# Windowed attention and a softplus FFN on one core: three score passes per head pair and query tile instead of four, and two buffers moved

## The chip, the cores and the metric

The kernel runs on one core of a Trainium2 chip. The metric is the device time of one execution in microseconds (us); lower is better. The engines are TensorE (PE in the profile; PEld are its weight loads), VectorE (DVE), ScalarE (ACT), GpSimd (POOL) and SyncE (SP), whose queue issues the DMAs. A pass is one matmul instruction: a weight load of up to 128 columns and a stream of moving columns over it.

## The reference

Attention over a causal window of 64 positions, followed by two matrix products with a softplus between them. Inputs are float32: q, k and v are (8, 8, 576, 64), that is 8 sequences, 8 heads, 576 positions, 64 per head; w_in is (512, 2048) and w_out (2048, 512).

```python
scores = scale * np.matmul(q, k.transpose(0, 1, 3, 2))
mask = (rel >= 0) & (rel < window)            # rel = query position - key position, window = 64
scores = np.where(mask, scores, -1000000000.0)
scores = scores - np.max(scores, axis=-1, keepdims=True)
attn = np.exp(scores)
attn = attn / (np.sum(attn, axis=-1, keepdims=True) + 1e-09)
attn_out = np.matmul(attn, v)
...
x = np.ascontiguousarray(attn_out.transpose(0, 2, 1, 3)).reshape(B * S, H * D)   # 4608 x 512
h = x @ w_in
g = np.maximum(h, 0.0) + np.log1p(np.exp(-np.abs(h)))
return (g @ w_out).astype(np.float32)
```

## The kernel before, in words

**Tiles.** The 4608 rows are cut into 12 blocks of 384 (TB), a block into 3 query tiles of 128 rows (NJ), the 8 heads into 4 head pairs of 2 x 64 = 128 rows of the transposed q and k. For a query tile only 192 keys can matter (W): 64 before it and its own 128.

**Two parts for one float32.** Most passes run on a type of 4 bytes that TensorE reads at less than float32's precision (fp32r). The kernel therefore writes a float32 value as an upper part (the value converted) and a lower part (the difference), and adds up the products of the parts that matter: upper x upper, upper x lower, lower x upper. The feed-forward passes (`ffn_up`, L401, and `ffn_down`, L422) do so with three passes for each product.

**Scores (L258).** In the first two blocks (`by_pe`) one float32 pass over a block diagonal of k (kbd, L113) gives the scores of both heads. In the ten later blocks q_hl holds, for each head of the pair, q's upper part in partitions 0 to 63 and q's lower part in 64 to 127 (L236, L237; q_in is loaded so that both halves hold the head). k_hi and k_lo (L242, L243) hold the head's k in both halves. One pass with q_hl of a head as weights and k_hi of the head as moving columns gives upper x upper + lower x upper; one with k_lo gives the terms with k's lower part. That is two passes of 192 columns for a head, four for a tile, 12 for a head pair of a block.

**After the scores.** VectorE adds the mask and takes the minimum (L265), folds the columns (L271), ScalarE takes the exponentials (L275), VectorE normalizes (L280 to L283). The weights are cut into bf16 parts (L303 to L311) and transposed by two DMAs (L307, L312) into tr. v is loaded into v_in (L318) and cut into three bf16 parts, v12 and v13 (L324, L325, L327, L328, L329). Then attention times v runs in short bf16 passes (L376), once for each head; the first half of a head's passes reads v12, the second v13. ScalarE and VectorE add the two halves of the result into xf (L381, L382), and xf is cut into x's two parts (L384, L385), which the feed-forward network of that block reads.

**Feed-forward.** For each of 16 slices of 128 hidden columns, `ffn_up` makes 12 passes of 384 columns into one of two PSUM tiles (ps_h), ScalarE and VectorE compute the softplus (L405, L406, L407, L409) and its two parts g (L411, L412); `ffn_down` makes 9 passes of 512 columns into the three output tiles.

**Order of the work.** `attention` is a generator that yields between its stages. Each stage of each head pair, each `ffn_up` and each `ffn_down` gets a due time, and all are emitted in the order of the due times (L448 to L478). Step n of the feed-forward network has 2n + 0.5 for its up part and 2n + 5.5 for its down part; 16 steps make a block, so a block has 32 units. A head pair of a late block starts 8 units after the one before it (SHP), and STG (L30) gives the times of its stages from there: -13 loads of q and k, -5.9 q_hl, -5 k_hi and k_lo, 0, 1, 2 the scores of the three tiles, 3 to 7 the softmax and the transposes, 7.1 the load of v_in, 12 and 14 its conversion, 16 and 17 attention times v for the two heads, xf and x. So the stages 16 and 17 of one head pair are due at 8 and 9 of the next. From due time 100 on TensorE runs in the order of emission; the order on the other engines and on SP's queue is made by the framework's scheduler, which need not keep it. The head pairs of block 2 (the third) start 7 units apart.

**Buffers.** Tiles with the same tag share a buffer, and the next tile of a tag waits until the last reader of the one before it is done. Here k_hi and k_lo take the tags k0 and k1 (shared with kbd), v_in the tag v_in (shared with the weights converted last, L160), xf the tag xf (shared with the identity matrix ident of the transposes, L140), q_hl the tag q_hl (shared with pt). Each has one buffer.

Of the kernel before, what the change touches and what calls it, by code (L numbers as in the profile page):

```python
# [8 lines left out]
F32 = mybir.dt.float32  # L9
BF16 = mybir.dt.bfloat16  # L10
F32R = mybir.dt.float32r
U32 = mybir.dt.uint32
AF = mybir.ActivationFunctionType
ALU = mybir.AluOpType

P = 128
TB = 384
NJ = TB // P
# [8 lines left out]
BASE = (-100, -10, 24)  # L27
PACE = (5, 4, 7)
STG0 = (-4.5, 0.5, 1, 2, 3, 4, 7, 8)
STG = (-13, -5.9, -5, 0, 1, 2, 3, 4, 5, 6, 7, 7.1, 12, 14, 16, 17)  # L30
SH, SHP = -12, 8
PE_ORDERED_FROM = 100
MANUAL = {mybir.EngineType.PE}
# [6 lines left out]
def window_attention_softplus_ffn(  # L40
# [7 lines left out]
    S: int,  # L48
    D: int,
):  # L50

# [13 lines left out]
    nc = tc.nc  # L65
# [13 lines left out]
    att = ctx.enter_context(tc.tile_pool(name="att", bufs=1))  # L79
# [29 lines left out]
    W = CH + P  # L109

    kbd_s = [att.tile([P, 2, CH + TB], F32, name="kbd", tag=f"k{i}") for i in range(2)]  # L113
    for t in kbd_s:
        nc.gpsimd.memset(t[D:P, 0, :], 0.0)
        nc.gpsimd.memset(t[0:D, 1, :], 0.0)
        nc.gpsimd.memset(t[0:D, 0, 0:CH], 0.0)
        nc.gpsimd.memset(t[D:P, 1, 0:CH], 0.0)

    v13 = cpool.tile([P, NCH, 2, 2, D], BF16, name="v13")  # L120
    v_ts = [att.tile([P, 2, NJ, P], F32, name="v_t", tag=n) for n in ("nat", "tr")]
    for t in v_ts:
        nc.gpsimd.memset(t[0:CH, 0, 0, :], 0.0)

# [12 lines left out]
    mask_c = cpool.tile([P, W], BF16, name="mask_c")  # L137
    nc.gpsimd.tensor_copy(mask_c, mask)
    nc.gpsimd.memset(mask_c[:, 0:CH], FAR)
    ident = att.tile([P, P], F32, name="ident", tag="xf")  # L140
    make_identity(nc, ident)

    mask_b = cpool.tile([P, W], BF16, name="mask_b")
# [4 lines left out]
    mm, tp = nc.tensor.matmul, nc.tensor.transpose  # L148
# [34 lines left out]
    def attention(g, hp):  # L183
# [36 lines left out]
        if by_pe:  # L220
            v_t = v_ts[hp % 2]

            def load_v(rows, lay, j0, j1, start):
                n = rows.stop - rows.start
                src = v[start + j0 * P : start + j1 * P, c0 : c0 + P].rearrange("(j p) n -> p j n", p=P)
                nc.sync.dma_start(v_t[rows, lay, j0:j1, :], src[:n, :, :])

            if t0 == 0:
                nc.sync.dma_start(v_t[CH:P, 0, 0, :], v[0:CH, c0 : c0 + P])
            load_v(slice(0, P), 0, 1 if t0 == 0 else 0, NJ, t0 - CH)  # L230
            load_v(slice(0, CH), 1, 0, NJ, t0 + CH)
            load_v(slice(CH, P), 1, 0, NJ, t0)
        else:
            q_hl = att.tile([P, 2, TB], F32R, name="q_hl")
            low = heads[1]
            nc.scalar.copy(q_hl, q_in)  # L236
            nc.vector.tensor_tensor(  # L237
                q_hl[low, :, :], q_in[low, :, :], q_hl[low, :, :].bitcast(F32), ALU.subtract
            )
            yield  # L240
            k_hi, k_lo = [att.tile([P, 2, W - P + TB], F32R, name=f"k{i}") for i in range(2)]
            nc.scalar.copy(k_hi, k_in)  # L242
            nc.vector.tensor_tensor(k_lo, k_in, k_hi.bitcast(F32), ALU.subtract)  # L243
        yield

        st = att.tile([P, 2, NJ, W], F32, name="st", bufs=2)
# [2 lines left out]
        for j in range(NJ):  # L249
            sp = bank()  # L250
            spv = sp[:, : 2 * W].rearrange("p (h c) -> p h c", h=2)
            js, kc = slice(j * P, (j + 1) * P), slice(j * P, j * P + W)
            if by_pe:
                mm(spv, qf[:, js], kf[:, :, kc], start=True, stop=True)  # L254
            else:
                for hh in range(2):
                    for i, part in enumerate((k_hi, k_lo)):
                        mm(  # L258
                            spv[:, hh, :], q_hl[:, hh, js], part[:, hh, kc],
                            start=(hh == 0 and i == 0), stop=(hh == 1 and i == 1), skip_group_check=True,  # L260
                        )
            t = ORDER[g] * NJ + j
            m = mask_c if (t * P) % S == 0 else mask_b if (t * P) % S + P > S else mask
            for hh in range(2):
                nc.vector.tensor_tensor_reduce(  # L265
                    st[:, hh, j, :], spv[:, hh, :], m, QSCALE, 3.0e38, ALU.add, ALU.min, mn[:, hh, j : j + 1]
                )
            yield
# [3 lines left out]
        for hh in range(2):  # L272
            for j in range(NJ):
                i = hh * NJ + j
# [8 lines left out]
        nc.vector.tensor_tensor(pn, pn, sm.unsqueeze(2).to_broadcast([P, 2 * NJ, P]), ALU.mult)  # L283
        if by_pe:

            pt = att.tile([P, 2, TB], F32, name="pt", tag="q_hl")
            for hh in range(2):
                pp = bank()
                for j in range(NJ):
                    tp(pp[:, j * P : (j + 1) * P], sv[:, hh * NJ + j, 0:P], ident)  # L290
                (nc.vector.tensor_copy if hh else nc.scalar.copy)(pt[:, hh, :], pp[:, :TB])
        else:

            nat = att.tile([P, 2, 4 * NJ, 2, CH], BF16, name="nat")
            tr = att.tile([P, 8 * NJ, P], BF16, name="tr")
# [14 lines left out]
            nc.vector.tensor_tensor(part(1, 0), pv[0], part(0, 1), ALU.subtract)  # L310
            nc.vector.tensor_copy(nat[:, 1, :, 1, :], nat[:, 0, :, 0, :])  # L311
            nc.sync.dma_start(  # L312
                tr[:, n:, :], nat[:, 1, :, :, :].rearrange("p n b c -> p (n b c)"), transpose=True
            )
            yield
            v_in = att.tile([P, NCH, P], F32, name="v_in")
            for half in heads:
                nc.sync.dma_start(v_in[half, :, :], v[ks, c0 : c0 + P].rearrange("(c p) n -> p c n", p=CH))  # L318
            yield

            v12 = att.tile([P, NCH, 2, 2, D], BF16, name="v12")
            vv = v_in.rearrange("p c (h d) -> p c h d", h=2)
            up, low = heads
            nc.scalar.copy(v12[:, :, :, 0, :], vv)  # L324
            nc.vector.tensor_tensor(vv, vv, v12[:, :, :, 0, :], ALU.subtract)  # L325
            yield
            nc.scalar.copy(v12[:, :, :, 1, :], vv)  # L327
            nc.vector.tensor_tensor(v13[low, :, :, 0, :], vv[low, :, :, :], v12[low, :, :, 1, :], ALU.subtract)  # L328
            nc.vector.tensor_copy(v13[up, :, :, 0, :], v12[up, :, :, 0, :])  # L329
# [8 lines left out]
        if by_pe:  # L338
            av = bank()
        else:  # L340
            xf = att.tile([P, TB], F32, name="xf")
            trf = tr.rearrange("p n t -> p (n t)")
        for hh in range(2):
            if by_pe:
                for a in range(2 * NJ):
# [3 lines left out]
                        start=(a == 0), stop=(a == 2 * NJ - 1), skip_group_check=True,  # L349
# [8 lines left out]
            for s in range(2):  # L358
                for c in range(0 if prev else 1, NCH):


                    j = (c - 1) // 2
                    n = s * 4 * NJ + (hh * NJ + j) * 2
# [11 lines left out]
            for i, (s, c, src, osl) in enumerate(passes):  # L375
                mm(  # L376
                    av[:, osl], (v13 if s else v12)[:, c, hh, :, :], src,
                    start=(i == 0), stop=(i == len(passes) - 1), skip_group_check=True,
# [12 lines left out]
    part = {}  # L391
# [131 lines left out]
```

## Time and profile before

| | |
|---|---|
| median of 3 runs | 1031.11 us (1030.70 to 1031.97) |
| the profiled execution, its own time | 1030.02 us |
| its span | 1028.2 us |
| mean granted TensorE clock | 0.976 |
| busy share of the span: PE, PEld, DVE, ACT, POOL | 95%, 84%, 78%, 72%, 6% |
| score passes L258 | 480 of 128x192, 76.5 us busy |
| feed-forward passes L401, L422 | 2304 and 1728, 445.3 and 435.5 us busy |
| attention times v, L376 | 1088 |

A row of instructions reads: line, engine, operation, written tile <- read tiles, shape and type, count, then busy time in us and the mean of one in ns, then the idle time of the engine just before them and what ended most of it. Matmuls overlap in time, so the mean of one pass is longer than the distance between the starts of two. A timeline row reads: start in us from the start of the span, duration in us, engine, line, operation, tiles, shape, and how many instructions the row merges. SPq is SP's queue, on which DMAs are issued. A row of waits reads: who waited for whom, us in total, times, the longest.

### The profile page before, as it was taken

Reading aid. Unit: us, or ns where it says so; the run is one execution under the profiler, and the core shown is the slowest. Engines: PE = TensorE matmul, PEld = TensorE weight load, DVE = VectorE, ACT = ScalarE, POOL = GpSimd, SP = SyncE. Lnnn points to the kernel's source line nnn. Section 1 sums busy time; section 2 is a strip of 40 time slices with the busy share of each in tenths; the row PEclk is TensorE's granted clock in tenths of the full one; section 3 lists DMA queues with packets and bytes.
Section 4 is the critical chain, followed back from the end, with each engine's and each line's share of the span. In section 5 each row is a group of like instructions: output and inputs, shape, how many; then the busy total and the mean of one; then the engine's idle time right before and its main releaser. Section 6 shows DMA issues by size and latency. Waiting matters only on the chain.

```text
span 1028.2 us, 16614 instructions
## 1 busy us (share of the span) xinstructions
PE 974.8 (95%) x5888; PEld 859.1 (84%) x5888; DVE 802.6 (78%) x1775; ACT 742.0 (72%) x1705; POOL 61.8 (6%) x56
## 2 busy tenths in 40 slices
PE   4559889999999999999999999999999999999998
PEld 2337778988888998998899899899989899889997
DVE  6998587797987888878878878878878887874332
ACT  5467477787877788778778778778878877865443
POOL 5365020000000000000000000000000000000000
PEclk8679989999999999999999999999999999999999
DMA  8662253375554456444444534534634635521000
GB/s 295 229 219 71 88 149 83 83 186 123 126 121 114 113 114 130 117 113 116 131 103 117 140 91 118 151 83 113 164 83 113 161 86 104 141 49 32 31 1 31
DMA packets 203155, 119.05 MB, mean 116 GB/s; under 512 B 130880, under 2 KB 195136, under 8 KB 201536
## 3 DMA queue, kind: packets, MB, share of 16 engines
q1 hardware_dynamic: 203072, 118.00, 45.4%
q8 instruction: 46, 0.75, 0.3%
q14 instruction: 37, 0.30, 0.1%
HBM read 76.28 MB, written 10.22 MB: 84 GB/s over the span
## 4 chain that ended last, share of the span: by engine, by line
PE 85%; DVE 9%; DMA 2%; ACT 1%; issue 1%; SPq 1%; DVEq 0%; ACTq 0%
PE ps_o L422 37%; PE ps_h L401 37%; PE ps_a L376 5%; PE ps_a L258 5%; DVE ws L172 2%; DVE ws L173 1%; DVE st L265 1%; DVE st L283 1%; DMA raws<-in_w_words_dram 1%; DVE ws L171 1%; DVE st L271 0%; DMA tr<-nat 0%; ACT st L275 0%; PE ps_a L254 0%; DVE sm L280 0%
## 5 line engine op out<-in xcount | busy, mean ns | idle before, releaser
L401 PE MATMUL ps_h<-x,w 128*128 128x384 f32 x2304 | 445.3, 340 | 7.6 <-ACT x L352 3.9
L422 PE MATMUL ps_o<-w,g 128*128 128x512 f32 x1728 | 435.5, 395 | 0.0
L401 PEld LDWEIGHTS ps_h<-x,w 128*128 128x128 f32 x2304 | 402.6, 189 | 22.5 <-ACT x L352 5.2
L422 PEld LDWEIGHTS ps_o<-w,g 128*128 128x128 f32 x1728 | 318.0, 188 | 57.7 <-ACT g L411 0.3
L405 ACT ACTIVATE u<-ps_h 128x384 f32<-128x384 f32 x192 | 93.9, 490 | 121.8 <-PE ps_h L401 118.8
L409 DVE SCALAR_TENSOR_TENSOR u<-ps_h,u 128x384 f32<-128x384 f32 x192 | 106.4, 554 | 70.5 <-ACT u L407 69.2
L275 ACT ACTIVATE st<-st,mn 128x128 f32<-128x128 f32 x288 | 111.9, 390 | 19.3 <-DVE st L271 19.3
L412 DVE TENSOR_TENSOR g<-u,g 128x384 fp32r<-128x384 f32 x192 | 106.6, 555 | 10.5 <-ACT g L411 8.6
L265 DVE CUSTOM_DVE_ANT_0 st<-ps_a,mask 128x192 f32<-128x192 f32 x216 | 69.4, 351 | 57.9 <-PE ps_a L258 45.4
L407 ACT ACTIVATE u<-u 128x384 f32<-128x384 f32 x192 | 100.3, 523 | 4.2
L406 ACT ACTIVATE u<-u 128x384 f32<-128x384 f32 x192 | 100.7, 526 | 3.2
L258 PE MATMUL ps_a<-k,q_hl 128*128 128x192 f32 x480 | 76.5, 283 | 0.0
L376 PEld LDWEIGHTS <-v 128*128 128x128 bf16 x1088 | 56.1, 98 | 22.9 <-issue 21.8
L376 PE MATMUL ps_a<-tr,v 128*128 128x128 bf16 (+1 forms) x1088 | 72.0, 213 | 0.2
L258 PEld LDWEIGHTS ps_a<-k,q_hl 128*128 128x128 f32 x480 | 66.6, 192 | 4.1 <-issue 0.5
L411 ACT CAST g<-u 128x384 fp32r<-128x384 f32 x112 | 57.0, 509 | 14.2 <-DVE u L409 13.5
L306 ACT CAST nat<-st 128x768 bf16<-128x768 f32 x40 | 33.2, 831 | 40.0 <-DVE st L304 40.0
L275 ACT ACTIVATION_READ_ACCUMULATOR st<-st,mn 128x1 f32 x288 | 53.9, 187 | 0.0
L381 ACT COPY xf<-ps_a 64x384 f32<-64x384 f32 x80 | 38.1, 477 | 20.3 <-PE ps_a L376 19.2
L283 DVE TENSOR_TENSOR st<-st,sm 128x768 f32<-128x768 f32 x48 | 47.6, 991 | 1.5
L382 DVE TENSOR_TENSOR xf<-ps_a,xf 64x384 f32<-64x384 f32 x80 | 43.9, 548 | 5.2 <-ACT xf L381 4.0
L325 DVE TENSOR_TENSOR v_in<-v_in,v 128x896 f32<-128x896 f32 x40 | 43.5, 1086 | 4.7 <-ACT v L324 4.7
(80 smaller groups left out, 868.0 us busy)
## 6 DMA issues: line engine op xcount, KB each, us to landing
k_in<-in_kT_dram SPq DMA_DIRECT2D x80, 224.0 KB, 3.9
v_in<-in_v_dram SPq DMA_DIRECT2D x80, 224.0 KB, 3.6
q_in<-in_qT_dram SPq DMA_DIRECT2D x84, 192.0 KB, 4.1
raws<-in_w_words_dram SPq DMA_DIRECT2D x12, 1024.0 KB, 6.0
out_dram<-raw SPq DMA_DIRECT2D x12, 512.0 KB, 2.8
raw<-in_w_words_dram SPq DMA_DIRECT2D x8, 512.0 KB, 4.3
out_dram<-raw SPq DMA_DIRECT2D x12, 256.0 KB, 2.6
v_t<-in_v_dram SPq DMA_DIRECT2D x16, 96.0 KB, 3.8
```

The lines of the kernel that those rows point to most:

```text
L258: mm(spv[:, hh, :], q_hl[:, hh, js], part[:, hh, kc], start=(hh == 0 and i == 0), stop=(hh == 1 and i == 1), skip_group_check=True,)
L265: nc.vector.tensor_tensor_reduce(st[:, hh, j, :], spv[:, hh, :], m, QSCALE, 3.0e38, ALU.add, ALU.min, mn[:, hh, j : j + 1])
L275: nc.scalar.activation(sv[:, i, 0:P], sv[:, i, 0:P], AF.Exp, bias=mn[:, hh, j : j + 1], scale=-1.0, accum_out=sm[:, i : i + 1])
L283: nc.vector.tensor_tensor(pn, pn, sm.unsqueeze(2).to_broadcast([P, 2 * NJ, P]), ALU.mult)
L376: mm(av[:, osl], (v13 if s else v12)[:, c, hh, :, :], src, start=(i == 0), stop=(i == len(passes) - 1), skip_group_check=True,)
L401: mm(hv, weight(0, a, f)[:, c * P : (c + 1) * P], x[b][c], start=(i_mm == 0), stop=(i_mm == 3 * NC - 1))
L405: nc.scalar.activation(u, hv, AF.Abs)
L406: nc.scalar.activation(u, u, AF.Exp, scale=-1.0)
L407: nc.scalar.activation(u, u, AF.Ln, bias=1.0)
L409: nc.vector.scalar_tensor_tensor(gf, hv, 0.0, u, ALU.max, ALU.add)
L412: nc.vector.tensor_tensor(gt[1], gf, gt[0].bitcast(F32), ALU.subtract)
L422: mm(ops[g][j], gt[a][:, js], weight(1, b, f), start=(first and i == 0), stop=(last and i == 2),)
```

## The change

k's lower part becomes a block diagonal. k_lo now has, for head 0, its lower part in partitions 0 to 63 and zeros in 64 to 127, and for head 1 the other way round. q_hl gets a third part: q's upper part of head 0 in partitions 0 to 63 and of head 1 in 64 to 127. One pass of 2 x 192 columns with that part as weights and k_lo as moving columns gives upper x lower of both heads; then one pass of 192 columns for each head with k_hi, as before. The product lower x lower, which the second pass of a head had in it, is no longer formed.

The zeros are written once, so k_lo is one tile for the whole kernel (tag k1), made by the first head pair that needs it. Its two nonzero quarters are written by two subtractions of 64 x 448 in place of one of 128 x 896. q_hl's third part is written by two ScalarE copies of 64 x 384.

q_hl grows from two parts to three. The buffer xf is given up: xf shares v_in's buffer, and ident lies in one of the two early v tiles (tag nat), which get one more column block. The load of v_in is emitted at 10.2 instead of 7.1.

```diff
-STG = (-13, -5.9, -5, 0, 1, 2, 3, 4, 5, 6, 7, 7.1, 12, 14, 16, 17)
+STG = (-13, -5.9, -5, 0, 1, 2, 3, 4, 5, 6, 7, 10.2, 12, 14, 16, 17)
...
+    k_los = []
...
-    v_ts = [att.tile([P, 2, NJ, P], F32, name="v_t", tag=n) for n in ("nat", "tr")]
+    v_tiles = [att.tile([P, 2 * NJ + 1, P], F32, name="v_t", tag=n) for n in ("nat", "tr")]
+    v_ts = [t[:, : 2 * NJ, :].rearrange("p (l j) n -> p l j n", l=2) for t in v_tiles]
...
-    ident = att.tile([P, P], F32, name="ident", tag="xf")
+    ident = v_tiles[0][:, 2 * NJ, :]
...
-            q_hl = att.tile([P, 2, TB], F32R, name="q_hl")
+            q_hl = att.tile([P, 3, TB], F32R, name="q_hl")
             low = heads[1]
-            nc.scalar.copy(q_hl, q_in)
+            nc.scalar.copy(q_hl[:, 0:2, :], q_in)
+            for hh, half in enumerate(heads):
+                nc.scalar.copy(q_hl[half, 2, :], q_in[half, hh, :])
...
-            k_hi, k_lo = [att.tile([P, 2, W - P + TB], F32R, name=f"k{i}") for i in range(2)]
+            k_hi = att.tile([P, 2, W - P + TB], F32R, name="k0")
             nc.scalar.copy(k_hi, k_in)
-            nc.vector.tensor_tensor(k_lo, k_in, k_hi.bitcast(F32), ALU.subtract)
+            if not k_los:
+                k_los.append(att.tile([P, 2, W - P + TB], F32R, name="k_lo", tag="k1"))
+                for hh, half in enumerate(heads):
+                    rest = heads[1 - hh]
+                    nc.vector.tensor_copy(
+                        k_los[0][rest, hh, :].rearrange("p (c d) -> p c d", d=D), v13[rest, :, hh, 1, :]
+                    )
+            k_lo = k_los[0]
+            for hh, half in enumerate(heads):
+                nc.vector.tensor_tensor(
+                    k_lo[half, hh, :], k_in[half, hh, :], k_hi[half, hh, :].bitcast(F32), ALU.subtract
+                )
...
+                mm(spv, q_hl[:, 2, js], k_lo[:, :, kc], start=True, stop=False, skip_group_check=True)
                 for hh in range(2):
-                    for i, part in enumerate((k_hi, k_lo)):
-                        mm(
-                            spv[:, hh, :], q_hl[:, hh, js], part[:, hh, kc],
-                            start=(hh == 0 and i == 0), stop=(hh == 1 and i == 1), skip_group_check=True,
-                        )
+                    mm(
+                        spv[:, hh, :], q_hl[:, hh, js], k_hi[:, hh, kc],
+                        start=False, stop=(hh == 1), skip_group_check=True,
+                    )
...
-            pt = att.tile([P, 2, TB], F32, name="pt", tag="q_hl")
+            pt = att.tile([P, 3, TB], F32, name="pt", tag="q_hl")
...
-            xf = att.tile([P, TB], F32, name="xf")
+            xf = att.tile([P, TB], F32, name="xf", tag="v_in")
```

More of the change, by code (lines that the diff above doesn't have):

```diff
@@ L233, in attention @@
         else:
-            q_hl = att.tile([P, 2, TB], F32R, name="q_hl")
+            q_hl = att.tile([P, 3, TB], F32R, name="q_hl")
             low = heads[1]
-            nc.scalar.copy(q_hl, q_in)
+            nc.scalar.copy(q_hl[:, 0:2, :], q_in)
+            for hh, half in enumerate(heads):
+                nc.scalar.copy(q_hl[half, 2, :], q_in[half, hh, :])
             nc.vector.tensor_tensor(
-                q_hl[low, :, :], q_in[low, :, :], q_hl[low, :, :].bitcast(F32), ALU.subtract
+                q_hl[low, 0:2, :], q_in[low, :, :], q_hl[low, 0:2, :].bitcast(F32), ALU.subtract
             )
             yield
-            k_hi, k_lo = [att.tile([P, 2, W - P + TB], F32R, name=f"k{i}") for i in range(2)]
+            k_hi = att.tile([P, 2, W - P + TB], F32R, name="k0")
             nc.scalar.copy(k_hi, k_in)
-            nc.vector.tensor_tensor(k_lo, k_in, k_hi.bitcast(F32), ALU.subtract)
+            if not k_los:
[10 more added lines that the diff above has]
+                )
         yield
```

## The prediction

> **What bounds the kernel now.** I read the page first (engine shares, costliest groups), then busy time by stretch, then the waits of the stretch in which the scores run, then the order of work in one head pair.
>
> ```profile
> span 1028.2 us, 16614 instructions
> PE 974.8 (95%) x5888; PEld 859.1 (84%) x5888; DVE 802.6 (78%) x1775; ACT 742.0 (72%) x1705; POOL 61.8 (6%) x56
> L258 PE MATMUL ps_a<-k,q_hl 128*128 128x192 f32 x480 | 76.5, 283 | 0.0
> 140.00:150.00 10.00, 9.77 (x51) 8.85 (x52) 9.94 (x21) 7.95 (x23) 3.19 (x2) 1.00 0.59 159
> 400.00:600.00 200.00, 200.00 (x1248) 180.16 (x1247) 169.17 (x389) 158.19 (x360) 0.00 (x0) 1.00 0.50 122
> PE ps_h L401 <- DVE u L409: 2.1, 3, 1.0
> ```
>
> The columns of the stretch rows are PE, PEld, DVE, ACT and POOL busy, then granted clock, DMA share and GB/s. In 400 to 600 us TensorE is busy without a gap at clock 1.00, VectorE for 169.17 of 200 us (85%) and ScalarE for 158.19 (79%). The last row belongs to the waits of TensorE from 100 us to the end: it waits three times for L409, 2.1 us in all; the other two rows of that view are single waits of the first two blocks. The kernel is therefore bound by TensorE's passes, and a pass that goes shortens the program by its pitch (the time from its start to the start of the next pass), as long as the other engines still deliver in time. The four score passes of a tile are the 480 of L258: 10 blocks of 384 rows, 4 head pairs, 3 tiles, 4 passes.
>
> **What a score pass costs.** Busy time is no pitch, since passes overlap. I take pitches from the timeline (start, duration, instruction):
>
> ```profile
> 513.48 0.67 PE L258 MATMUL ps_a<-k,q_hl 128*128 128x192 f32 x4
> 513.99 2.29 PE L401 MATMUL ps_h<-x,w 128*128 128x384 f32 x12
> 519.36 0.59 PE L258 MATMUL ps_a<-k,q_hl 128*128 128x192 f32 x4
> 519.78 2.27 PE L401 MATMUL ps_h<-x,w 128*128 128x384 f32 x12
> 521.89 2.24 PE L422 MATMUL ps_o<-w,g 128*128 128x512 f32 x9
> ...
> 499.86 0.59 PE L258 MATMUL ps_a<-k,q_hl 128*128 128x192 f32 x4
> 499.95 0.50 PE L258 MATMUL ps_a<-k,q_hl 128*128 128x192 f32 x3
> 500.06 0.39 PE L258 MATMUL ps_a<-k,q_hl 128*128 128x192 f32 x2
> 500.28 0.36 PE L401 MATMUL ps_h<-x,w 128*128 128x384 f32 x1
> 499.97 0.30 PEld L258 LDWEIGHTS ps_a<-k,q_hl 128*128 128x128 f32 x2
> 500.08 0.19 PEld L258 LDWEIGHTS ps_a<-k,q_hl 128*128 128x128 f32 x1
> 500.20 0.19 PEld L401 LDWEIGHTS ps_h<-x,w 128*128 128x128 f32 x1
> 502.39 2.24 PE L422 MATMUL ps_o<-w,g 128*128 128x512 f32 x9
> 504.47 2.27 PE L401 MATMUL ps_h<-x,w 128*128 128x384 f32 x12
> ```
>
> Twelve passes of 384 columns take 519.78 to 521.89, so 2.11/12 = 0.176 us each; nine of 512 columns take 502.39 to 504.47, so 0.231 us. Four score passes of 192 columns take 0.42 us where they follow a wide pass (499.86 to 500.28, 519.36 to 519.78) and 0.51 us where they follow the short bf16 passes of attention times v (513.48 to 513.99). Inside a group the weight loads start at 499.97, 500.08 and 500.20, so 0.11 us apart, and each pass follows its own load by 0.09 (499.97 to 500.06). So narrow passes come at the pace of their weight loads, 0.11 us, except one whose load ran under a longer pass: that one follows after 0.09 (499.86 to 499.95).
>
> **The change, part by part.** *The passes.* Before, 4 x 192 = 768 columns on four weight loads; after, 384 + 192 + 192 = 768 columns on three. No column goes; one weight load does. After a wide pass: 0.176 for the 384-column pass, which hides the next load; 0.09 for the first narrow pass; 0.11 for the last: 0.376 instead of 0.42, so 0.046 us saved. After bf16 passes the group begins with a load that nothing hides; that is 0.51 - 0.42 = 0.09 in both kernels, so 0.46 instead of 0.51, 0.05 saved. Per head pair one tile is of the first kind and two of the second: 0.046 + 2 x 0.05 = 0.146, rounded down to 0.14 us; over 40 head pairs **5.6 us**. Bounds: if two narrow passes cost their mean, 0.21, against one at 0.176, 0.034 x 120 = 4.1 us. If the wide pass costs what the difference of the two wide pitches says, (0.231 - 0.176)/128 = 0.43 ns a column, 0.165 us, then 0.22 - 0.165 = 0.055, so 6.6 us. I take 5.6, for its rows are the group itself.
>
> The Trainium skill has a rule that speaks against this, on the page "TensorE: Matmul & The Clock Gate", section "Back-to-back issue gap": an isolated pass is spaced N/2.4 + 2.5 ns, 82.5 ns at 192 columns and 162.5 at 384. By that one 384-column pass equals two of 192 but for 2.5 ns, and my estimate from it would be 0.3 us for 120 tiles. The rows above disagree: four passes took 420 ns at best, not 330.
>
> *ScalarE* gains two copies of 64 x 384 per head pair, the third part of q_hl. *VectorE* makes k's lower part in two pieces of 64 x 448 instead of one of 128 x 896. *The buffers*: xf now shares v_in's buffer, and the load of v_in is emitted at 10.2, not 7.1.
>
> ```profile
> L384 ACT CAST x<-xf 128x384 fp32r<-128x384 f32 x40 | 20.3, 508 | 0.9 <-DVE xf L382 0.7
> L243 DVE TENSOR_TENSOR k<-k_in,k 128x896 fp32r<-128x896 f32 x40 | 43.4, 1085 | 0.0
> L412 DVE TENSOR_TENSOR g<-u,g 128x384 fp32r<-128x384 f32 x192 | 106.6, 555 | 10.5 <-ACT g L411 8.6
> L283 DVE TENSOR_TENSOR st<-st,sm 128x768 f32<-128x768 f32 x48 | 47.6, 991 | 1.5
> L329 DVE COPY v<-v 64x896 bf16<-64x896 bf16 x40 | 15.2, 379 | 0.1
> ```
>
> ScalarE: 2 x 0.508 = 1.02 us a head pair. A head pair takes 519.36 - 499.86 = 19.5 us, in which ScalarE is busy 15.4; 16.4 of 19.36 is 85%. VectorE: between 555 ns at 384 elements and 991 at 768 a piece of 448 costs 0.63; two are 1.26, 0.17 more than 1.085; its share goes from 85% to 86%. Both fit under TensorE, so I cost them at nothing in the steady stretch; what is late if they don't is a rival below. Once, k_lo's zero halves are filled by two VectorE copies of 64 x 448, between 0.2 (half of L329) and 0.63 us each. They and the first q copies fall near 120 to 150 us, where TensorE is not full (9.77 of 10 in the row above) and VectorE is (9.94). I take 0.8 us there, bounds 0 (hidden) and 2 x 0.63 + 1.02 = 2.3. The ident tile's move changes no instruction: nothing.
>
> *v_in's load on SP's queue* passes only the output stores of a block's end (emitted at 3.5 of each 32, the load now at 6.2 instead of 3.1). Its new wait is the last reader of xf, L385 of the head pair before; behind it on SP stand the next loads of k_in and q_in, which in the rows of rival A issue right after it (502.78, 504.64, 505.97) and are converted in the next head pair, 19.5 us after the L243 and L237 shown there.
>
> Sum against the profiled execution (1030.02 us, span 1028.2): 1030.02 - 5.6 + 0.8 = 1025.2. It lies 1.1 below the median of the runs, 1031.11, so **1026.3 us**.
>
> **Rivals.** *A, v arrives too late (slower).*
>
> ```profile
> 512.85 0.79 PE L376 MATMUL ps_a<-tr,v 128*128 128x128 bf16 x12
> 516.71 0.93 ACT L324 CAST v<-v_in 128x896 bf16<-128x896 f32 x1
> 518.02 1.09 DVE L325 TENSOR_TENSOR v_in<-v_in,v 128x896 f32<-128x896 f32 x1
> 519.02 0.38 DVE L329 COPY v<-v 64x896 bf16<-64x896 bf16 x1
> 519.14 0.94 ACT L327 CAST v<-v_in 128x896 bf16<-128x896 f32 x1
> 521.16 1.09 DVE L328 TENSOR_TENSOR v<-v_in,v 64x896 bf16<-64x896 f32 x1
> ...
> 502.78 1.29 SPq L318 DMA_DIRECT2D v_in<-in_v_dram  x2
> 503.52 1.08 DVE L243 TENSOR_TENSOR k<-k_in,k 128x896 fp32r<-128x896 f32 x1
> 504.64 1.24 SPq L215 DMA_DIRECT2D k_in<-in_kT_dram  x2
> 504.64 0.95 DVE L237 TENSOR_TENSOR q_hl<-q_in,q_hl 64x768 fp32r<-64x768 f32 x1
> 505.63 0.56 DVE L385 TENSOR_TENSOR x<-xf,x 128x384 fp32r<-128x384 f32 x1
> 505.97 2.08 SPq L212 DMA_DIRECT2D q_in<-in_qT_dram  x2
> 506.10 0.55 DVE L412 TENSOR_TENSOR g<-u,g 128x384 fp32r<-128x384 f32 x1
> 506.58 2.24 PE L422 MATMUL ps_o<-w,g 128*128 128x512 f32 x9
> ...
> v_in<-in_v_dram SPq DMA_DIRECT2D x80, 224.0 KB, 3.6
> ```
>
> Before, v_in is loaded at 502.78, and converted from 516.71 to 522.25 for a pass that starts at about 532. After, the chain is: L385, load, L324, L325, L327, L328, then the passes with v13, the second half of L376's twelve (512.85 to 513.48), so from 513.15. The load takes half its issue, 0.65, and 3.6 to land: 4.25. The four conversions are 0.93 + 1.09 + 0.94 + 1.09 = 4.05. If the queue keeps its order, L385 ends at 505.63 + 0.56 + 0.17 = 506.36, L328 at 506.36 + 4.25 + 4.05 = 514.66, and TensorE waits 1.5 us in every head pair: 40 x 1.5 = 60 us, about 1086. It decides from the point where L385 ends later than 513.15 - 8.3 = 504.85; a wait of 0.14 us a head pair already eats the whole gain. Against it: the conversions themselves, L325, L329 and L328 (1.09 + 0.38 + 1.09 = 2.56 us), now stand in front of L385 (one head pair later: 518.02, 519.02, 521.16 against 525.13) and must move behind it. Then L385 ends near 506.36 - 2.56 = 503.8, and 1.05 us is left for queueing in four hops; 3 us, if L385 also goes ahead of L243 and L237 (1.08 + 0.95), neither of which it needs. That is enough, but not much: **chance 0.26**.
>
> *B, the saving is eaten (no change).* Two ways, together **0.13**. First, passes cost by columns: at 0.43 ns a column below 0.176, a 192-column pass is 0.093 and two are 0.186 against 0.176, which gives 0.010 x 120 = 1.2 us, about 1030; the loads 0.11 apart speak against it. (The skill's rule above is this case.) Second, VectorE delivers later: L412 ends at 506.65, and the down pass that needs it is the third from 506.58, at 507.04; 0.39 us are left, and L243 takes 0.17 of it. If the moved conversions take it all and 0.14 more, the time is that of before, about 1031. The same 2.56 us that leave this stretch speak against it.
>
> *C, the change doesn't do what it says*: the block diagonal streams its zero halves too, so columns stay at 768; that is counted above and is why I forecast half a per cent and not a quarter of the scores' time.
>
> **How the numbers follow.** The forecast has 0.61, A 0.26, B 0.13. A measurement of this kernel tells about 0.2% (2 us) from no change. Forecast and its bounds (4.1 to 6.6 saved, 0 to 2.3 in the transition) give 1024.5 to 1029.3; earlier L385 at block ends may add a little, so the low end is 1023.8. The high end goes into A as far as a wait of 0.4 us a head pair: 1026.3 + 16 = 1042, which leaves out most of A's longer waits. The forecast's own range is 1023.8 to 1029. Faster 0.61, same 0.13, slower 0.26.
>
> **What would show it.** L258 with 360 passes, 120 of them 128x384. Groups of three in 0.38 us after a wide pass and 0.46 after bf16 ones, and 19.36 us from head pair to head pair with TensorE full from 200 to 940 us. L385 ahead of the v_in load, L328 done before 513 in the frame above. Wrong if L376 waits for L324 or L328 (rival A), if L422 waits for L412 (B), or if groups of three take as long as four.

## The result, and the profile after

The changed kernel takes 1099.69 us (median of 4 runs, 1099.48 to 1100.03) against 1030.9 us for the kernel before: a ratio of 1.0669, 95% interval 1.065 to 1.0687. It is 68.8 us slower, where the prediction had 1026.3 and a range up to 1042. The profiled execution took 1099.9 us, span 1098.0.

The page after, and busy time from 400 to 600 us (columns as before):

```profile
span 1098.0 us, 16625 instructions
PE 988.8 (90%) x5768; PEld 853.9 (78%) x5768; DVE 812.5 (74%) x1817; ACT 776.8 (71%) x1785; POOL 61.4 (6%) x56
L272 PE MATMUL ps_a<-k_lo,q_hl 128*128 128x384 f32 x120 | 46.9, 394 | 2.1 <-DVE k_lo L257 1.1
...
400.00:600.00 200.00, 187.77 (x1131) 163.69 (x1130) 156.33 (x367) 151.69 (x345) 0.00 (x0) 1.00 0.42 108
```

The passes are as announced: 120 wide ones and, in another row, 240 narrow ones. But TensorE, busy for all of 200 us before, is now busy for 187.77, and VectorE and ScalarE are busy for less of the stretch than before too. No engine is full: everything waits for something. The waits from 400 to 600 us name it (who waited for whom, us in total, times, longest):

```profile
PEld ps_h L417 <- DVE u L425: 11.8, 9, 1.3
PEld ps_o L438 <- DVE g L428: 8.3, 9, 0.9
PE ps_h L417 <- DVE u L425: 7.9, 9, 0.9
PE ps_o L438 <- DVE g L428: 4.4, 9, 0.5
```

Lines have moved by 3 at the loads, 5 to 16 further down: L417 is the up pass (L401 before), L425 the VectorE step that ends the softplus and frees the up pass's PSUM tile (L409 before). The up pass waits for it nine times, which is once in every head pair of the stretch. The down pass (L438) waits nine times too, for L428, which writes the lower part of g (L412 before). No pass waits for v there. Rows from the timeline of one head pair show how a slice's softplus comes late:

```profile
511.89 0.34 PE L272 MATMUL ps_a<-k_lo,q_hl 128*128 128x384 f32 x1
512.12 0.55 DVE L401 TENSOR_TENSOR x<-xf,x 128x384 fp32r<-128x384 f32 x1
512.27 2.27 PE L417 MATMUL ps_h<-x,w 128*128 128x384 f32 x12
512.70 1.28 SPq L334 DMA_DIRECT2D v_in<-in_v_dram  x2
513.21 1.03 ACT L241 CAST q_hl<-q_in 64x384 fp32r<-64x384 f32 x2
514.26 0.94 ACT L247 CAST k<-k_in 128x896 fp32r<-128x896 f32 x1
514.38 2.24 PE L438 MATMUL ps_o<-w,g 128*128 128x512 f32 x9
515.23 0.49 ACT L421 ACTIVATE u<-ps_h 128x384 f32<-128x384 f32 x1
517.16 0.52 ACT L422 ACTIVATE u<-u 128x384 f32<-128x384 f32 x1
518.35 0.93 ACT L340 CAST v<-v_in 128x896 bf16<-128x896 f32 x1
519.18 0.52 ACT L423 ACTIVATE u<-u 128x384 f32<-128x384 f32 x1
519.79 1.08 DVE L341 TENSOR_TENSOR v_in<-v_in,v 128x896 f32<-128x896 f32 x1
521.10 0.54 DVE L425 SCALAR_TENSOR_TENSOR u<-ps_h,u 128x384 f32<-128x384 f32 x1
521.69 2.35 PE L417 MATMUL ps_h<-x,w 128*128 128x384 f32 x12 [0.88 <-DVE u L425]
522.81 1.09 DVE L344 TENSOR_TENSOR v<-v_in,v 64x896 bf16<-64x896 f32 x1
523.88 0.63 PE L438 MATMUL ps_o<-w,g 128*128 128x512 f32 x2
524.40 0.55 DVE L428 TENSOR_TENSOR g<-u,g 128x384 fp32r<-128x384 f32 x1
525.00 1.90 PE L438 MATMUL ps_o<-w,g 128*128 128x512 f32 x7 [0.49 <-DVE g L428]
```

The slice that ends at 514.38 waits 0.85 us for ScalarE, which is still at the copies (L241) and k_hi (L247). Then four exponentials go ahead of its second step and two more, with v's first conversion L340, ahead of its third, L423. On VectorE L341 goes ahead of L425. From the slice's end to the end of L425 pass 7.26 us (514.38 to 521.64). The lateness of this one slice stops TensorE twice: at 521.69 the up pass has waited for its PSUM tile, and at 525.00 the down group has stopped after two passes, because L428 of the same slice runs behind L344. The same slice before:

```profile
522.10 0.49 ACT L405 ACTIVATE u<-ps_h 128x384 f32<-128x384 f32 x1
524.70 0.51 ACT L407 ACTIVATE u<-u 128x384 f32<-128x384 f32 x1
526.07 0.55 DVE L409 SCALAR_TENSOR_TENSOR u<-ps_h,u 128x384 f32<-128x384 f32 x1
```

Its passes ended at 521.89, so that was 4.73 us. The up pass that reuses the tile comes after a down, an up and a down group, some 6.3 us later (2.09 + 2.11 + 2.08, the mean times of such groups before): 4.73 fits, 7.26 doesn't. The chain that ended last, which was 85% TensorE before, has 34% TensorE, 16% VectorE and 13% ScalarE now; from one head pair:

```profile
513.21 0.51 ACT q_hl L241
513.73 0.51 ACT q_hl L241
514.26 0.94 ACT k L247
515.23 0.49 ACT u L421
515.73 1.52 ACT st L291 x8
...
519.79 1.08 DVE v_in L341
520.87 0.23 issue
521.10 0.54 DVE u L425
```

**Where the time came from.** The start of an up slice is a good marker: the 49th slice (the fourth block's first) starts at 327.83 us before and at 345.56 after, 17.7 us later; the 169th, 30 head pairs on, at 915.93 and 985.06, 69.1 us later. So two losses add up: **17.7 us up to the fourth block** and **1.71 us in each head pair after it**. The scores themselves gained what was predicted: the mean time from the first pass of a group to the pass behind it, over 400 to 900 us, fell from 0.508 to 0.457 and 0.462 after bf16 passes and from 0.422 to 0.377 after wide ones, 0.142 us a head pair. Over the same stretch the two down groups of a head pair that an up group follows grew from 2.080 to 2.596 us on the mean, 1.03 us for both, and the down group ahead of attention times v from 2.089 to 2.835, 0.75 us. These two waits, less the saving, are the 1.71 us but for 0.07.

The early loss has another part besides the waits. Rows from the third block, of the passes and of one stretch of 4 us:

```profile
263.76 0.62 PE L417 MATMUL ps_h<-x,w 128*128 128x384 f32 x2 [3.23 <-ACT x L400]
268.77 4.21 PE L417 MATMUL ps_h<-x,w 128*128 128x384 f32 x12 [1.88 <-DVE u L425]
272.78 3.13 PE L438 MATMUL ps_o<-w,g 128*128 128x512 f32 x9
275.75 1.73 PE L417 MATMUL ps_h<-x,w 128*128 128x384 f32 x9
268.00:272.00 4.00, 3.23 (x10) 3.23 (x11) 2.52 (x5) 1.90 (x4) 0.00 (x0) 0.50 0.78 215
```

The first up pass waits 3.23 us for x. From about 264.5 to 274.7 us the granted clock is 0.50, and from start to start twelve up passes take 4.01 us and nine down passes 2.97, where 2.11 and 2.08 are usual at clock 1.00: 2.8 us more in these two groups alone.

### The profile page after: what moved, and what is told of

Read it like the earlier page. It is cut to its first block, busy times and chain, and to the rows that moved or that the text cites. A ratio compares the mean times of both kernels' runs of the same rounds, so it can differ in the third digit from the quotient of the medians.

```text
span 1098.0 us, 16625 instructions
## 1 busy us (share of the span) xinstructions
PE 988.8 (90%) x5768; PEld 853.9 (78%) x5768; DVE 812.5 (74%) x1817; ACT 776.8 (71%) x1785; POOL 61.4 (6%) x56
## 4 chain that ended last, share of the span: by engine, by line
PE 34%; DVE 16%; ACT 13%; issue 6%; DMA 2%; SPq 0%; ACTq 0%
PE ps_o L438 15%; PE ps_h L417 11%; ACT st L291 6%; PE ps_a L392 4%; DVE u L425 3%; DVE v_in L341 3%; DVE v L344 3%; ACT q_hl L241 3%; ACT k L247 2%; DVE st L320 2%; PE ps_a L272 2%; DMA v_in<-in_v_dram 2%; PE ps_a L274 2%; DVE g L428 2%; ACT u L421 1%
## 5 line engine op out<-in xcount | busy, mean ns | idle before, releaser
L417 PE MATMUL ps_h<-x,w 128*128 128x384 f32 x2304 | 451.6, 343 | 45.2 <-DVE u L425 36.2
L417 PEld LDWEIGHTS ps_h<-x,w 128*128 128x128 f32 x2304 | 404.1, 190 | 73.4 <-DVE u L425 52.4
L438 PE MATMUL ps_o<-w,g 128*128 128x512 f32 x1728 | 442.8, 397 | 15.3 <-DVE g L428 14.4
L438 PEld LDWEIGHTS ps_o<-w,g 128*128 128x128 f32 x1728 | 317.1, 188 | 84.7 <-DVE g L428 27.7
L421 ACT ACTIVATE u<-ps_h 128x384 f32<-128x384 f32 x192 | 93.3, 487 | 152.0 <-PE ps_h L417 104.5
L425 DVE SCALAR_TENSOR_TENSOR u<-ps_h,u 128x384 f32<-128x384 f32 x192 | 106.3, 554 | 61.6 <-ACT u L423 59.3
L428 DVE TENSOR_TENSOR g<-u,g 128x384 fp32r<-128x384 f32 x192 | 107.9, 562 | 16.5 <-ACT g L427 12.7
L281 DVE CUSTOM_DVE_ANT_0 st<-ps_a,mask 128x192 f32<-128x192 f32 x216 | 68.8, 352 | 59.2 <-PE ps_a L274 46.8
L423 ACT ACTIVATE u<-u 128x384 f32<-128x384 f32 x192 | 100.7, 524 | 3.2
L422 ACT ACTIVATE u<-u 128x384 f32<-128x384 f32 x192 | 100.1, 522 | 3.3
L427 ACT CAST g<-u 128x384 fp32r<-128x384 f32 x112 | 57.0, 509 | 33.6 <-DVE u L425 33.4
L392 PE MATMUL ps_a<-tr,v 128*128 128x128 bf16 (+1 forms) x1088 | 68.6, 213 | 0.8 <-ACT v L343 0.8
L296 DVE TENSOR_SCALAR sm<-sm 128x6 f32<-128x6 f32 x48 | 10.4, 216 | 72.2 <-ACT st L291 72.2
L341 DVE TENSOR_TENSOR v_in<-v_in,v 128x896 f32<-128x896 f32 x40 | 43.5, 1086 | 14.9 <-ACT v L340 14.8
L257 DVE TENSOR_TENSOR k_lo<-k_in,k 64x448 fp32r<-64x448 f32 x80 | 49.6, 620 | 3.1 <-ACT k L247 1.8
L239 ACT CAST q_hl<-q_in 128x768 fp32r<-128x768 f32 x40 | 33.5, 836 | 24.4 <-PE ps_a L274 24.4
L272 PE MATMUL ps_a<-k_lo,q_hl 128*128 128x384 f32 x120 | 46.9, 394 | 2.1 <-DVE k_lo L257 1.1
```

The costliest lines, as they stand in the source:

```text
L272: mm(spv, q_hl[:, 2, js], k_lo[:, :, kc], start=True, stop=False, skip_group_check=True)
L281: nc.vector.tensor_tensor_reduce(st[:, hh, j, :], spv[:, hh, :], m, QSCALE, 3.0e38, ALU.add, ALU.min, mn[:, hh, j : j + 1])
L392: mm(av[:, osl], (v13 if s else v12)[:, c, hh, :, :], src, start=(i == 0), stop=(i == len(passes) - 1), skip_group_check=True,)
L417: mm(hv, weight(0, a, f)[:, c * P : (c + 1) * P], x[b][c], start=(i_mm == 0), stop=(i_mm == 3 * NC - 1))
L421: nc.scalar.activation(u, hv, AF.Abs)
L422: nc.scalar.activation(u, u, AF.Exp, scale=-1.0)
```

## The experiments

The table gives, for each kernel, the median, its ratio to the kernel before with its interval, and by how much the 49th and the 169th up slice start later than before. These starts come from one execution of each kernel; the executions of the kernel before reach from 1029.17 to 1032.78 us, so differences of 2 us or so between them are not told apart.

| kernel | us | ratio (95%) | 49th | 169th |
|---|---|---|---|---|
| changed | 1099.69 | 1.0669 (1.065 to 1.0687) | +17.7 | +69.1 |
| e1 buffers only | 1049.22 | 1.0178 (1.0162 to 1.0194) | +17.6 | +19.7 |
| e2 three passes, xf in raw | 1042.07 | 1.0109 (1.0094 to 1.0124) | +16.8 | +12.5 |
| e3 changed, copies on GpSimd | 1048.73 | 1.0173 (1.0155 to 1.0191) | +18.3 | +18.0 |
| e4 as e2, copies on GpSimd | 1050.35 | 1.0191 (1.0176 to 1.0206) | +19.6 | +20.9 |
| e5 changed, logarithm first | 1046.15 | 1.015 (1.0136 to 1.0163) | +15.1 | +16.2 |
| e6 changed, three PSUM tiles | 1125.79 | 1.0919 (1.0904 to 1.0934) | +25.9 | +94.3 |
| e7 three passes, xf in st | 1040.21 | 1.0085 (1.0071 to 1.0099) | +13.3 | +7.9 |
| e8 as e7, copies on GpSimd | 1039.25 | 1.0083 (1.0069 to 1.0097) | +7.7 | +8.3 |
| e9 as e7, TensorE in order from 60 | 1028.96 | 0.9983 (0.9974 to 0.9991) | +4.3 | -1.3 |
| e10 as e7, logarithm first | 1035.13 | 1.0048 (1.0036 to 1.0061) | +4.0 | +5.1 |
| e11 as e5, TensorE in order from 60 | 1050.32 | 1.0191 (1.0178 to 1.0205) | +20.2 | +20.1 |
| e12 before, TensorE in order from 60 | 1031.6 | 1.0005 (0.9996 to 1.0015) | +1.8 | +1.7 |
| e13 as e10, TensorE in order from 60 | 1032.95 | 1.0018 (1.0009 to 1.0027) | +3.8 | +3.8 |
| e14 as e1, TensorE in order from 60 | 1057.74 | 1.0259 (1.0245 to 1.0274) | +24.3 | +27.7 |
| e15 as e7, TensorE in order from 30 | 1032.4 | 1.0012 (1.0002 to 1.0021) | +7.9 | +2.4 |

**e1: the buffers alone.** The kernel before with the diff's lines for v_tiles, ident, xf's tag and 10.2, and four score passes.

> Four score passes as before; only xf moves into v_in's buffer, ident into the early v tile, and v_in's load to 10.2. Theory Q (queue): the shared buffer alone moves v's conversion behind x, into the stretch where it stands ahead of the softplus of a slice in ScalarE's and VectorE's queues, and the up passes wait for their PSUM tile; then this kernel loses 1 to 2 us a head pair, 1070 to 1105 us. Theory L (load): the 1.19 us that ScalarE and VectorE get in addition are what makes the softplus late; then this kernel stays at 1031 us. Theory S (sum): only both together are too much; then 1031 to 1045 us.

Measured: 1049.22 us. That is between the theories, nearest to S: the buffers alone lose 17.6 us before the fourth block and 2 us in the 30 head pairs behind it. The kernel before in 240 to 300 us, then this run in 240 to 300 and 400 to 600 us:

```profile
240.00:300.00 60.00, 60.00 (x376) 53.17 (x376) 50.71 (x112) 48.30 (x110) 0.00 (x0) 1.00 0.51 119
...
240.00:300.00 60.00, 51.65 (x317) 44.98 (x316) 50.37 (x115) 43.15 (x99) 0.00 (x0) 0.91 0.62 136
400.00:600.00 200.00, 199.75 (x1246) 179.99 (x1245) 165.65 (x382) 158.29 (x367) 0.00 (x0) 1.00 0.51 122
```

So the buffers alone bring an early loss, and the full steady loss needs the rest of the change too.

**e2: three passes without the shared buffer.**

```diff
-STG = (... 7, 10.2, 12, ...)
+STG = (... 7, 7.1, 12, ...)
-            xf = att.tile([P, TB], F32, name="xf", tag="v_in")
+            xf = ff.tile([P, 1, DM], w_words.dtype, name="raw").bitcast(F32)[:, 0, 0:TB]
```

> Three score passes as in the changed kernel, but v_in keeps its buffer and its load stays at 7.1; xf goes into the two buffers named raw, which in the late blocks only the output rows use. Theory Q: 1026 us, the predicted saving of 5.6 us and little else. Theory L: 1080 to 1100 us, since ScalarE's two copies and VectorE's two pieces are all there. Theory S: 1026 to 1035 us.

Measured: 1042.07 us. There is no steady loss: from the 49th to the 169th slice it gains 4.3 us, 0.14 a head pair, the predicted saving, with ScalarE's copies in place. But 16.8 us are lost before. The two buffers named raw also take the partial output rows of the first block; whether that is the reason isn't shown: between 200 and 345 us ScalarE waits for a store out of raw only once, for 0.9 us. e7 puts xf elsewhere.

**e3: the changed kernel with the copies on GpSimd.**

```diff
-                nc.scalar.copy(q_hl[half, 2, :], q_in[half, hh, :])
+                nc.gpsimd.tensor_copy(q_hl[half, 2, :], q_in[half, hh, :])
```

> The changed kernel with the two copies of q's upper part on GpSimd, which has nothing to do in the late blocks, instead of on ScalarE. Theory Q: the order around the softplus stays, 1075 to 1100 us, at best 1 us a head pair less than the changed kernel. Theory L: 1025 to 1035 us. Theory S: 1025 to 1035 us.

Measured: 1048.73 us. With 1.02 us a head pair taken off ScalarE the steady loss is gone (18.3 and 18.0); the early loss stays. But the order on ScalarE is another one too: in the changed kernel L340 stands ahead of the logarithm of the slice above in all 29 head pairs of the steady stretch, here in 8 of them. Together with e5 below this gives all four cases, as the time from the slice's end to the end of its softplus step on VectorE (median, with the number of head pairs):

| | logarithm ahead of v's first conversion | conversion ahead of the logarithm |
|---|---|---|
| copies on GpSimd | 4.30 us (e3, 21) | 6.14 us (e3, 8) |
| copies on ScalarE | 5.96 us (e5, 29) | 7.26 us (changed, 29) |

The up pass that reuses the tile comes 6.27 us after the slice's end where nothing is late (the median of the kernel before). So either one alone still fits, if barely (two of the eight, at 6.53 and 6.79 us, don't), and the two together never do. That is theory S for the steady loss; the early loss puts e1, e2 and e3 above its ranges all the same.

**e4: e2 with the copies on GpSimd**, the same edit.

> Three score passes with v_in's own buffer as in the second run, and the two copies on GpSimd. Theory Q: 1025 us, about as the second run, since ScalarE's 1.02 us were hidden. Theory L: 1025 us, and some 60 us less than the second run. Theory S: 1025 us.

Measured: 1050.35 us, 8 us more than e2: another start (19.6), and no steady saving. All three theories had 1025. Moving the copies is no cure in itself; why it gives no steady saving here wasn't followed up.

**e5: the place of v's first conversion.** The changed kernel with L340 queued behind the last logarithm:

```diff
-        nc.scalar.activation(u, u, AF.Ln, bias=1.0)
+        last_ln[:] = [nc.scalar.activation(u, u, AF.Ln, bias=1.0)]
...
-            nc.scalar.copy(v12[:, :, :, 0, :], vv)
+            with tc.issue_after(last_ln[0].ins):
+                nc.scalar.copy(v12[:, :, :, 0, :], vv)
```

> The changed kernel; the one edit is that v's first conversion on ScalarE (L340) is queued behind the softplus logarithm (L423) that was emitted last before it. Theory P (place in the queue): in the steady blocks the changed kernel's 21.3 us a head pair come from L340 and what follows it standing ahead of the softplus of a slice, so that the up pass waits for its PSUM tile; with the order turned round a head pair takes about 19.45 us, and only the loss of about 17 us at the start of the third and fourth block stays: 1041 to 1050 us. Theory W (work): ScalarE and VectorE have too much to do with the shared buffer and the copies, in whatever order; then 1085 to 1100 us.

Measured: 1046.15 us, as theory P said. With all the work of the changed kernel in place the steady loss is gone (15.1 and 16.2). So the same work fits in another order. The edit moved more than one instruction, though: with it v's second conversion stands behind the next slice's logarithm, and on VectorE the softplus step and g's lower part go ahead of the subtractions for v (L343, L346), where the changed kernel had them behind. The same slice in its timeline, where the logarithm is L425, v's first conversion L342, the up pass L419 and the softplus's last step L427:

```profile
499.07 2.24 PE L440 MATMUL ps_o<-w,g 128*128 128x512 f32 x9
499.93 0.49 ACT L423 ACTIVATE u<-ps_h 128x384 f32<-128x384 f32 x1
503.04 0.52 ACT L425 ACTIVATE u<-u 128x384 f32<-128x384 f32 x1
503.45 0.93 ACT L342 CAST v<-v_in 128x896 bf16<-128x896 f32 x1
504.49 0.55 DVE L427 SCALAR_TENSOR_TENSOR u<-ps_h,u 128x384 f32<-128x384 f32 x1
505.34 2.27 PE L419 MATMUL ps_h<-x,w 128*128 128x384 f32 x12
```

The slice ends at 499.07, L427 at 505.04: 5.97 us, under the 6.3 there are, and the up pass starts without a wait. The saving of the three passes isn't seen in it, though: the down group ahead of attention times v takes 2.27 us on the mean, 2.09 before, and that eats 0.18 us a head pair.

**e6: a third PSUM tile for the up passes**, one less for scores and attention times v.

```diff
-tc.tile_pool(name="ps_a", bufs=3, ...    tc.tile_pool(name="ps_h", bufs=2, ...
+tc.tile_pool(name="ps_a", bufs=2, ...    tc.tile_pool(name="ps_h", bufs=3, ...
```

> The changed kernel with three PSUM tiles for the up passes (ps_h) and two instead of three for scores and attention times v (ps_a). Theory P: the up pass no longer waits for the softplus two slices back; unless ps_a becomes a wait of its own, 1040 to 1060 us. Theory W: the softplus falls behind all the same, 1085 to 1100 us.

Measured: 1125.79 us, worse than both theories. In 400 to 600 us the up pass no longer waits; the down pass does, for the same slices' last VectorE step, 12.0 us in nine times:

```profile
PE ps_o L438 <- DVE g L428: 12.0, 9, 1.3
```

So the late softplus stops TensorE also where the up pass has a tile to spare: ps_h is only the first place where it shows. With two edits in one (ps_a has one less) it tells no more.

**e7 and e8: three passes, no shared buffer.** xf lies in the 384 columns of the next head pair's score tile that the fold leaves unread:

```diff
+        sts[g * NP + hp] = st
...
-            xf = att.tile([P, TB], F32, name="xf", tag="v_in")
+            xf = sts.get((g * NP + hp) + 1, st).rearrange("p h j c -> p (h j) c")[:, :, P:]
...
-STG = (... 7, 10.2, 12, ...)
+STG = (... 7, 7.1, 12, ...)
```

> Three score passes with v_in's own buffer and its load at 7.1; xf lies in the 384 columns of the next head pair's score tile st that nobody reads after the fold (L287), so it shares no buffer with a load. If the loss at the third and fourth block comes from shared buffers (v_in with xf, or raw with xf), it goes, and with it the steady saving of 0.15 us a head pair is left: 1024 to 1028 us. If ScalarE's extra copies make that loss, 1038 to 1045 us stays.

> As e7, with the two copies of q's upper part on GpSimd. If the shared buffers made the loss, 1024 to 1028 us, as e7. If the copies made it, this one is at 1024 to 1028 us and e7 at 1038 or more. GpSimd's copies may hold up VectorE: the run with them in e4 took 8 us more than e2; then 1030 to 1036 us.

Measured: 1040.21 and 1039.25 us. e7 lies in the range given for the copies as the cause, but e8, without them on ScalarE, is hardly faster and lies in none of its ranges. e7 has the steady saving (13.3 to 7.9, 0.18 us a head pair), e8 does not, and both lose at the start, 13.3 and 7.7 us. So there is an early loss without a shared buffer too. Before due time 100 the scheduler orders TensorE too, and e7's timeline has two up groups in a row there, 24 passes (L421), behind a wait for the softplus (L429):

```profile
268.72 6.01 PE L421 MATMUL ps_h<-x,w 128*128 128x384 f32 x24 [2.00 <-DVE u L429]
```

**e9, e12, e15: TensorE in the order of emission from 60 or 30 on, not from 100.**

```diff
-PE_ORDERED_FROM = 100
+PE_ORDERED_FROM = 60        # e15: 30
```

> As e7 (three passes, xf in st, no shared buffer), but TensorE runs in the order of emission from due time 60 on instead of 100. Theory F (free order): the 13 us that e7 lost up to the end of the third late block come from the order that the scheduler gave TensorE before due time 100, another one in each kernel; then they go, and with the steady saving 1025 to 1030 us. Theory D (delivery): ScalarE and VectorE deliver late there in any order; then 1037 to 1045 us.

> The kernel before with TensorE in the order of emission from due time 60. Theory F: the order that the scheduler chose for the kernel before has next to no waits there, so that an order of emission gains nothing, 1030 to 1034 us. Theory D: the same.

> e9 with TensorE in the order of emission from due time 30 instead of 60. e9 loses some 4 us before its third block. If that is the free order up to 60, 1024 to 1028 us; if ScalarE's and VectorE's added work in the change of blocks, 1028 to 1033 us.

Measured: e9 1028.96, e12 1031.6, e15 1032.4 us. e9 is theory F: the loss at the start falls from 13.3 to 4.3 us and the saving comes behind it, 5.6 us in 30 head pairs. Its ratio of 0.9983 (0.9974 to 0.9991) is 2 us under the kernel before, which is no more than the prediction said can be told apart. Against e12, the kernel before with the same order on TensorE, it is 2.6 us faster. Its busy times:

```profile
400.00:600.00 200.00, 200.00 (x1239) 180.36 (x1238) 171.73 (x400) 167.33 (x382) 0.00 (x0) 1.00 0.49 119
```

TensorE is full again, with ScalarE at 84% and VectorE at 86%. e12 shows that the kernel before gains nothing from this order. e15 loses 7.9 us at the start, so the last 4 us of e9 are not to be had by fixing the order between 30 and 60 as well.

**e10: e7 with e5's edit.**

> As e7, with v's first conversion queued behind the last softplus logarithm, as in e5. Theory F: the loss up to the third late block stays or changes at random with the order, 1030 to 1045 us. Theory D: the softplus comes earlier, 1026 to 1032 us.

Measured: 1035.13 us, inside theory F's range. The start is as good as e9's (4.0), with the scheduler's order on TensorE, so that order is not bad in every kernel. But the steady saving is gone, by the same 2.27 us down group as in e5 (2.272 here). Putting the logarithm first has its own price.

**e11, e13, e14: is it the shared buffer?** e11 is e5 with TensorE in order from 60; e13 is e11 with xf in st and v_in's load at 7.1; e14 is e1 with TensorE in order from 60.

> The changed kernel with both: L340 behind the logarithm as in e5, and TensorE in the order of emission from due time 60. Theory F: of the 16 us that e5 still lost 10 or more go, 1030 to 1037 us. Theory D: 1043 to 1050 us, since the shared buffer makes x late there in any order.

> e11 but for the buffer: three passes, L340 behind the logarithm, TensorE in the order of emission from 60, xf in st instead of in v_in's buffer, and v_in's load at 7.1. Theory D (the shared buffer makes v and x late at the start of the late blocks, whatever TensorE's order): 1029 to 1036 us, 15 us or more under e11. Theory F (only orders chosen by the scheduler): near e11, 1045 to 1052 us.

> Four passes, xf in v_in's buffer with its load at 10.2 (e1), TensorE in the order of emission from 60. Theory D: the loss of e1 stays, 1043 to 1053 us. Theory F: it goes, as it did from e7 to e9, 1029 to 1035 us.

Measured: e11 1050.32, e13 1032.95, e14 1057.74 us. e13 is where theory D had it; e11 and e14 lie a little above its ranges and far from theory F's. With the buffer shared the order of emission is no help, and it shows what the buffer costs: from e11 to e13, which differ in xf's place and the due time of the load alone, 17.4 us go, and from e14 to e12, which differ in the buffers and that due time alone, 26.1 us. In e11, where TensorE can't turn to other work, the rows of one head pair are rival A's chain (L403 is x's last step, L335 the load of v_in, L342 to L345 v's conversion, L394 attention times v):

```profile
246.19 0.55 DVE L403 TENSOR_TENSOR x<-xf,x 128x384 fp32r<-128x384 f32 x1
246.76 1.27 SPq L335 DMA_DIRECT2D v_in<-in_v_dram  x2
251.47 0.94 ACT L342 CAST v<-v_in 128x896 bf16<-128x896 f32 x1 [1.22 <-DMA v_in<-in_v_dram]
252.44 1.09 DVE L343 TENSOR_TENSOR v_in<-v_in,v 128x896 f32<-128x896 f32 x1 [2.66 <-ACT v L342]
253.57 0.94 ACT L345 CAST v<-v_in 128x896 bf16<-128x896 f32 x1
254.56 0.82 PE L394 MATMUL ps_a<-tr,v 128*128 128x64 bf16 x7 [5.39 <-ACT v L345]
```

x is done at 246.74 and the load issues at 246.76, so here it waits for the buffer and not for its due time. v is there at about 251.4, L345 ends at 254.51 and the passes start at 254.56, after a wait of 5.39 us.

For the early loss of the changed kernel this leaves two causes, of which either can be enough: without the shared buffer 13.3 us are lost (e7), with it and TensorE in order 20.2 (e11), and with neither about 4 (e9, e13).

## Why the prediction was wrong

- *The saving of the passes* was right: 5.6 us predicted; 0.142 us a head pair measured in the groups themselves, 5.7 over 40, and 5.6 us over 30 head pairs in e9, which includes a little beside the scores. Narrow passes at the pace of their weight loads, and one load less, fit it. Rival B's first form (passes cost by columns) is out. So is, for such a group, the spacing that the Trainium skill's page "TensorE: Matmul & The Clock Gate", section "Back-to-back issue gap", gives for an isolated pass, and for that alone: by it a group would have gained 2.5 ns, and it gained 45 to 51.
- *"Both fit under TensorE, so I cost them at nothing in the steady stretch"* is the step that failed. Shares of 85% and 86% do fit, as e2, e7 and e9 show with the same work. But the cover was read from averages over a head pair. The place that decides is one slice: its softplus had 4.73 us where about 6.3 are to be had, 1.5 us of slack, and the copies, L340 and L341 in front of it make 7.26. The copies alone or the conversion alone would have fitted (5.96 and 6.14); the sum was put at nothing and cost 1.71 us a head pair. I looked for such slack at L412 (0.39 us) and at v's chain, not at the PSUM tile that L409 frees.
- *Rival B's second form*, VectorE late with g's lower part, was priced at no change. Its sign, L422 waiting for L412 (now L438 for L428), is there nine times from 400 to 600 us, one down group later than the one that B looked at, and it is 0.75 us of the loss.
- *Rival A* named the right part of the change and nearly its price (1086), by a mechanism that does not act in the steady blocks; that the price came near is luck. As argued against it, L385 (now L401) moved ahead of L242 and L257 (L237 and L243 before), the v_in load issues at 512.70, L344 ends at 523.90, and attention times v starts at about 526.7: 2.8 us to spare, where I had 3. What I did not follow is where the conversions went: away from 516.7 to 522.3 and into the time in which a softplus is due. "Must move behind it" was counted as a relief of one place and not as a load of the next.
- *The transition* was put at 0.8 us, at most 2.3, for the added copies. It cost 17.7. The shared buffer alone brings that much (17.6 in e1): there rival A's chain does act, x comes late, and the granted clock falls to 0.50 for about 10 us. The order that the scheduler gives TensorE before due time 100 can bring 13.3 without it (e7), though not in e10. The sum had neither. The head pairs of the third block follow at 7 units and not 8, which I had in the text of the code and not in the sum; no run tries what that does. e9, e10 and e13, without the shared buffer, put what is left at about 4 us; e12, without any of the added work, has 1.8.
- The chance of 0.26 for slower was too low, and the range ended at 1042 because I let A's longer waits fall out of it.

Two things stay open. Why the scheduler puts L340 ahead of the logarithm in every head pair of the changed kernel, in 8 of 29 in e3 and in 6 of 29 in e1, was not tried. And what the 4 us at the start of e9 are was not settled.

## What to carry to other kernels

When a buffer is shared, the work that waits for it moves; cost it at the place where it lands, and look there for the buffers with the least slack, which may belong to another loop. A full engine's cover is as good as the slack of the slice with the least of it, not the share that is free on the average. Where an order is made by a scheduler, an edit of half a per cent can change the order and with it the time by six: keep the order of the critical engine fixed while you measure, and try the place of single instructions before you judge the edit.

## What the runs showed of the hardware

GpSimd's copies of 64 x 384 took 531 ns each in e8, against 509 on ScalarE in the changed kernel, so the idle engine did them at about the same price (spans on GpSimd are rough in these profiles). The pieces of 64 x 448 on VectorE took 620 ns, close to the 630 worked out from neighbouring sizes.

Where TensorE had stood idle for several microseconds, its granted clock fell to 0.50 for a while: in the changed kernel after a wait of 3.23 us, for about 10 us, and in e11 during a wait of 5.14 us, for about 17 us. In the kernel before, e9 and e13, whose longest single wait of TensorE from 200 to 345 us is 1.6 us, it stayed at 1.00 there. That the waits brought the lower clock is inferred from this; no run tries it by itself.
